# Hashed attention with spatial gating: the scores of two heads at once, each in 64 rows of the PE array, without copies of split q and k, and a part of the last batch's feed-forward sums moved ahead

## The chip, the cores and the metric

The kernel runs on one core of a Trainium2 chip. Its engines work side by side, each through its own instructions in order: TensorE (PE, with its weight loads shown apart as PEld), VectorE (DVE), ScalarE (ACT), GpSimd (POOL) and SyncE (SP), which here only issues DMAs. The time is device microseconds for one execution; lower is better. A profile is one execution taken apart.

## The reference, cut to what matters

```python
# attention: B=4, H=8, S=768, D=64
q_bucket, k_bucket = sign bits of q @ proj, k @ proj        # 6 bits each
mask = q_bucket[:, :, :, None] == k_bucket[:, :, None, :]
scores = where(mask, q @ k.T / 8, -1e9)
attn = softmax(scores)                                      # over the keys
x = (attn @ v) of all heads, side by side                   # B x 768 x 512
# feed-forward with spatial gating: d_ff = 1024
h = relu(x @ w_in);  u, v = halves of h
v_n = (v - mean(v)) / sqrt(var(v) + 1e-6)
v_s = w_spatial @ v_n + b_spatial                           # over the sequence
out = (u * v_s) @ w_out
```

## The kernel before, in words

Precision is kept by splitting: q, k, v, x and the weights each become a float16 high part and a float16 rest, and a product is made of three float16 products (high by high, high by rest, rest by high). The mask is part of the score product: the six hash bits of a query and a key and their complements are extra rows of the contraction, scaled so that a key of another bucket gets a score far below the others.

The work is counted in heads n = 0 to 31 (two heads are a pair p = n // 2, eight heads a batch) and in row tiles i = 0 to 5 of 128 rows. One head step g = 6n + i is one row tile of one head.

For each pair q and k are loaded (`load_qk`, L149), the hash bits are made by four matmuls in four column strips of the array (`hash_rows`, L168), and the split parts are written to `hl` (`split_qk`, L185), with the two heads of the pair in partitions 0 to 63 and 64 to 127. `build` (L193) then copies, by DMA, the parts of one head into a tile `ab` of its own, so that all 128 rows are used in a contraction: one matmul takes the rest of q over the high part of q, against the high part of k over the rest of k, and the other takes the high parts over the hash rows. The big copies (L199, L205, L211, L212) go to SP's queue, the small ones of the hash bits (L201) to SP's for the first batch and to ACT's queue later.

`scores` (L278) does a head step for queries in rows: four matmuls of 384 columns into a PSUM tile of two banks (L291, L292), the row minimum of the negated scores on DVE (L293), the exponential on ACT (L295), the split of the result into `pp` (L298 on ACT, L299 on DVE or POOL), and a DMA transpose to `pt` on SP's queue (L301). Heads 1 to 7 (`KEYS`, L451) instead have the keys in rows (`scores_k`, L256), which needs no transpose; for that the row maxima are found ahead of time (`row_max`, L235: two matmuls and a maximum on DVE) and put into the hash rows. The PSUM pool for both, `ps_sc` (L67), holds two tiles. `weighted` (L303) multiplies by v a few head steps later (`LAG` 5, `LAGK` 3), `normalize` (L318) ends a head, and `transpose_x` (L341) turns the pair's result into `xt`.

When a batch's eight heads are done, `mlp_units` (L350) puts 28 units in a queue: six for v, then for each half of the sequence four for u, four for the spatial product s and three for the output. Each unit is one PSUM tile of 12 or 18 matmuls. The main loop (L504 to L569) takes 28 units from the queue over 48 head steps of the next batch; after the last head step, the rest is emitted in a row (L572). The weights are converted bit by bit over the first 73 head steps (`W_PTS`, L456).

The order on each engine is set by the scheduler, from the priorities that `at(g, k)` (L485) gives to what is emitted.

Of the kernel before, what the change touches and what calls it, by code (L numbers as in the profile page):

```python
# [19 lines left out]
P = 128  # L20
# [16 lines left out]
def lsh_attention_spatial_gating(  # L37
# [22 lines left out]
    VYB = 2  # L60
# [21 lines left out]
    NAB = 4  # L82
    NR = D + 2 * NB
    ab = [const.tile([P, 4, S], F16, name=f"ab{i}") for i in range(NAB)]
    for i, t in enumerate(ab):
        eng = nc.vector if i % 2 else nc.gpsimd
        eng.memset(t[D:P, 2:4, :], 0.0)
        eng.memset(t[96:P, 2, :], HK)
# [76 lines left out]
    def has_keys(p):  # L165
        return 2 * p in KEYS or 2 * p + 1 in KEYS

    def has_queries(p):  # L168
        return not (2 * p in KEYS and 2 * p + 1 in KEYS)

    def hash_rows(p):
# [11 lines left out]
        st["sg", p] = s1  # L183

    def split_qk(p):  # L185
        qk = st["qk", p]
        hl = wk.tile([P, 4, S], F16, tag="hl", bufs=1, name=f"hl{p}")
# [4 lines left out]

    def build(n):  # L193
        p, e = divmod(n, 2)
        hl, sg, t = st["hl", p], st["sg", p], ab[n % NAB]
        r = slice(D * e, D * e + D)
        q_s, q_h = (BQ_S[n >= NH], BQ_H[n >= NH])
        if n < 1:
            nc.sync.dma_start(out=t[0:D, 2:4], in_=hl[r, 1:3])  # L199
        for j in range(4):  # L200
            q_s.dma_start(  # L201
                out=t[D:NR, 3 - j // 2, (j % 2) * HS:(j % 2 + 1) * HS],
                in_=sg[32 * j + 16 * e:32 * j + 16 * e + 2 * NB, :])
        if n < 1:
            q_h.dma_start(out=t[0:D, 0:2], in_=hl[r, 0:2])  # L205
        else:

            top = hl[r, 0:2]
            (ps, pn), (ss, sn), (es, en) = top.ap
            src = replace(top, ap=[(ps, pn), (ss, 2), (ss, 2), (es, en)])  # L210
            q_h.dma_start(out=t[0:D].rearrange("p (a b) s -> p a b s", b=2), in_=src)  # L211
        q_h.dma_start(out=t[D:P, 0:2], in_=hl[r, 2:4])  # L212
# [8 lines left out]
    def mean_v(p):  # L221
# [6 lines left out]
        nc.gpsimd.tensor_add(c, c, a[:, 4:6])  # L228
        mp = ps_m.tile([P, 512], F32, tag=MT, name=f"mp{p}")
# [5 lines left out]
    def row_max(n, i):  # L235
        t = ab[n % NAB]
        if i == 0:
            st["mx", n] = wk.tile([P, NT], F32, tag="mx", bufs=2, name=f"mx{n}")
        ps = ps_sc.tile([P, 2, 512], F32, tag="sc", name=f"mp{n}_{i}")[:, :, :HS]
        for c in range(2):  # L240
            nc.tensor.matmul(ps[:, c], lhsT=t[0:P - 1, 3, i * P:(i + 1) * P],
                             rhs=t[0:P - 1, 2, c * HS:(c + 1) * HS], start=True, stop=True)
        nc.vector.reduce_max(st["mx", n][:, i:i + 1], ps, axis=AX.XY)
        if i == NT - 1:
            nb = st["nb", n] = wk.tile([P, NT], F32, tag="nb", bufs=3, name=f"nb{n}")
# [8 lines left out]
            MQ.dma_start(out=t[P - 1:P, 3, :], in_=mt)  # L254

    def scores_k(n, i):  # L256
        t = ab[n % NAB]
        ps = ps_sc.tile([P, 2, 512], F32, tag="sc", name=f"sp{n}_{i}")[:, :, :HS]
        ks = slice(i * P, (i + 1) * P)
        for c in range(2):  # L260
            cs = slice(c * HS, (c + 1) * HS)
            nc.tensor.matmul(ps[:, c], lhsT=t[:, 1, ks], rhs=t[:, 0, cs], start=True, stop=False)  # L262
            nc.tensor.matmul(ps[:, c], lhsT=t[:, 2, ks], rhs=t[:, 3, cs], start=False, stop=True)  # L263
        ex = wk.tile([P, S], F32, tag="pt", bufs=PTB, name=f"ex{n}_{i}")
        st["ex", n, i] = nc.scalar.activation(ex.rearrange("p (c q) -> p c q", c=2), ps, AF.Exp, scale=ISQ).ins
        st["pt", n, i] = ex
# [11 lines left out]
    def scores(n, i):  # L278
        if n in KEYS:
            scores_k(n, i)  # L280
            return
        t = ab[n % NAB]
        if i == 0:
            st["nb", n] = wk.tile([P, NT], F32, tag="nb", bufs=3, name=f"nb{n}")
        nb = st["nb", n][:, i:i + 1]
        jk = wk.tile([P, 2, HS], BF16, tag="jk", name=f"jk{n}_{i}")
        qs = slice(i * P, (i + 1) * P)
        ps = ps_sc.tile([P, 2, 512], F32, tag="sc", name=f"sp{n}_{i}")[:, :, :HS]
        for c in range(2):
            cs = slice(c * HS, (c + 1) * HS)  # L290
            nc.tensor.matmul(ps[:, c], lhsT=t[:, 0, qs], rhs=t[:, 1, cs], start=True, stop=False)  # L291
            nc.tensor.matmul(ps[:, c], lhsT=t[0:P - 1, 3, qs], rhs=t[0:P - 1, 2, cs], start=False, stop=True)  # L292
        nc.vector.tensor_scalar(jk, ps, -ISQ, None, op0=ALU.mult, op1=ALU.min, accum_out=nb)  # L293
        ex = wk.tile([P, 2, HS], F32, tag="ex", bufs=EB, name=f"ex{n}_{i}")
        st["ex", n, i] = nc.scalar.activation(ex, ps, AF.Exp, bias=nb, scale=ISQ).ins  # L295
        at(NT * n + i + G_H, 50)
        pp = wk.tile([P, 2, 2, HS], F16, tag="pp", bufs=PB, name=f"pp{n}_{i}")
        nc.scalar.copy(pp[:, 0], ex)  # L298
# [4 lines left out]
    def weighted(n, i):  # L303
        if n in KEYS:
            weighted_k(n, i)
            return
# [307 lines left out]
```

## Time and profile before

| | us |
|---|---|
| median of 3 runs | 740.14 (740.12 to 741.45) |
| the profiled execution | 743.49 |
| its span, first to last instruction | 741.7 |
| PE, DVE, ACT, POOL busy in it | 631.5, 520.6, 434.8, 321.2 |

Busy time is the union of an engine's instructions. PE's matmuls overlap, and each is shown with its latency, so that a busy PE need not be at its peak. The granted clock is the share of TensorE's full clock that it was given. The chain of waits is followed back from the last instruction to what released it at each step. A line of a group reads: line, engine, operation, output<-input, shapes, count, then busy time in all, the mean in ns, and the idle time ahead of it with what ended that. DMAs in the chain are named by output<-input.

### The profile page before, as it was taken

To read this page: it belongs to the slowest core of one execution; us is meant where nothing else is said; L and a number is where in the kernel's file an instruction comes from. 1 tells how busy PE (TensorE), PEld (TensorE's weight loads), DVE (VectorE), ACT (ScalarE), POOL (GpSimd) and SP (SyncE) were. 2 spreads that over 40 slices of the span, in tenths; PEclk is the share of its full clock that TensorE was granted. 3 is DMA by queue.
4 is the path that set the end of the run, shared out by engine and by line. 5 is a ranking of instruction groups with operands and counts; after the bars stand their busy time and mean duration, and the time that the engine had idled before them with its cause. 6 is when DMAs were issued, how large, how long until landed. Compare 5 with 4: busy or idle time off the path is not lost.

```text
span 741.7 us, 14927 instructions
## 1 busy us (share of the span) xinstructions
PE 631.5 (85%) x5759; PEld 400.4 (54%) x5759; DVE 520.6 (70%) x945; ACT 434.8 (59%) x668; POOL 321.2 (43%) x324
## 2 busy tenths in 40 slices
PE   1569898998988776997898899889898998999997
PEld 0237686776445444554544555556455565654553
DVE  4677795536799999567689798678698987755200
ACT  1344574346788676655676577667677776743221
POOL 5122443123458675264314565156235571451503
PEclk9768797999999989898999999999999999999999
DMA  9565554324999989996999799999999999860011
GB/s 235 149 123 155 133 148 102 99 55 97 224 237 197 215 207 187 213 178 138 234 202 199 138 210 213 211 211 212 206 210 181 194 175 213 182 136 15 1 42 43
DMA packets 290011, 120.95 MB, mean 163 GB/s; under 512 B 270740, under 2 KB 273812, under 8 KB 289940
## 3 DMA queue, kind: packets, MB, share of 16 engines
q1 hardware_dynamic: 287636, 119.11, 76.4%
q10 hardware_dynamic: 2304, 0.89, 0.5%
q8 instruction: 45, 0.74, 0.4%
q14 instruction: 26, 0.21, 0.1%
HBM read 28.33 MB, written 6.29 MB: 47 GB/s over the span
## 4 chain that ended last, share of the span: by engine, by line
PE 43%; DMA 21%; DVE 13%; issue 8%; ACT 6%; POOL 6%; SPq 3%; ACTq 0%; DVEq 0%; POOLq 0%
DMA pt<-pp 14%; PE pv L275 6%; PE vps L361 6%; PE ops L432 5%; PE sps L417 5%; PE ups L402 5%; DMA ab<-hl 4%; PE sp L291 3%; DVE jk L293 3%; PE sp L292 3%; DVE pp L299 2%; PE sp L262 2%; PE pv L314 2%; ACT ex L295 2%; PE sp L263 2%
## 5 line engine op out<-in xcount | busy, mean ns | idle before, releaser
L295 ACT ACTIVATE ex<-sp,nb 128x768 f32<-128x768 f32 x150 | 134.1, 897 | 54.8 <-DVE jk L293 48.9
L299 DVE TENSOR_TENSOR pp<-ex,pp 128x768 f16<-128x768 f32 x116 | 126.2, 1089 | 47.6 <-ACT pp L298 46.5
L293 DVE TENSOR_SCALAR_CACHE_REDUCE jk<-sp 128x768 bf16<-128x768 f32 x150 | 142.4, 949 | 24.1 <-PE sp L292 22.2
L298 ACT CAST pp<-ex 128x768 f16<-128x768 f32 x150 | 124.3, 829 | 50.0 <-DMA pt<-pp 43.9
L314 PE MATMUL pv<-vp,pt 128*128 128x65 f16 x900 | 108.2, 198 | 40.5 <-DMA pt<-pp 40.2
L291 PE MATMUL sp<-ab 128*128 128x384 f16 x300 | 103.2, 344 | 31.6 <-ACT ex L295 19.3
L314 PEld LDWEIGHTS <-pt 128*128 128x128 f16 x900 | 86.7, 101 | 67.2 <-DMA pt<-pp 53.4
L299 POOL TENSOR_TENSOR pp<-ex,pp 128x768 f16<-128x768 f32 x34 | 58.1, 1708 | 131.1 <-ACT pp L298 124.6
L315 PE MATMUL pv<-vp,pt 128*128 128x64 f16 x900 | 108.0, 197 | 0.0
L316 PE MATMUL pv<-vp,pt 128*128 128x65 f16 x900 | 107.8, 198 | 0.0
L292 PE MATMUL sp<-ab 127*128 127x384 f16 x300 | 103.9, 346 | 0.0
L417 PE MATMUL sps<-ws,vn 128*128 128x384 f16 x576 | 100.9, 329 | 1.5 <-DVE sg L180 1.0
L315 PEld LDWEIGHTS <-pt 128*128 128x128 f16 x900 | 87.0, 100 | 11.3 <-issue 1.3
L316 PEld LDWEIGHTS <-pt 128*128 128x128 f16 x900 | 86.9, 100 | 3.1 <-issue 0.5
L417 PEld LDWEIGHTS <-vn 128*128 128x128 f16 x576 | 55.3, 99 | 37.8 <-issue 3.9
L432 PE MATMUL ops<-wo,g 128*128 128x512 f16 x288 | 70.9, 391 | 1.5 <-ACT o L436 0.9
L275 PEld LDWEIGHTS pv<-vf,ex 128*128 128x128 f32 x504 | 68.5, 208 | 4.1 <-issue 1.6
L402 PE MATMUL ups<-xt,wi 128*128 128x384 f16 x384 | 69.1, 333 | 1.3 <-ACT u L405 0.9
L361 PE MATMUL vps<-wi,xt 128*128 128x512 f16 x288 | 68.0, 383 | 1.4 <-DMA xt<-xs 1.3
L275 PE MATMUL pv<-vf,ex 128*128 128x65 f32 x504 | 67.0, 286 | 0.0
L333 POOL TENSOR_TENSOR x<-x,xf 128x384 f32<-128x384 f32 x32 | 35.5, 1110 | 64.1 <-DVE x L332 64.1
L422 POOL TENSOR_TENSOR sy<-sy,u 128x384 f32<-128x384 f32 x32 | 36.6, 1145 | 49.3 <-DVE sy L421 49.2
(87 smaller groups left out, 1010.7 us busy)
## 6 DMA issues: line engine op xcount, KB each, us to landing
qk<-kq SPq DMA_DIRECT2D x16, 768.0 KB
ab<-hl SPq DMA_DIRECT2D x31, 384.0 KB
ab<-hl SPq DMA_DIRECT2D x34, 192.0 KB
out<-o SPq DMA_DIRECT2D x24, 256.0 KB
v<-v SPq DMA_DIRECT2D x13, 384.0 KB
raw<-w_in SPq DMA_DIRECT2D x16, 256.0 KB
pt<-pp SPq DMA_TRANSPOSE x150
raw<-w_sp SPq DMA_DIRECT2D x12, 192.0 KB
```

The source lines that it names most:

```text
L275: nc.tensor.matmul(acc[:, qi, :], lhsT=ex[:, qi * P:(qi + 1) * P], rhs=vf[p % 2][:, 2 * i + e, :], start=(i == 0 and qi == 0), stop=(i == ...
L291: nc.tensor.matmul(ps[:, c], lhsT=t[:, 0, qs], rhs=t[:, 1, cs], start=True, stop=False)
L292: nc.tensor.matmul(ps[:, c], lhsT=t[0:P - 1, 3, qs], rhs=t[0:P - 1, 2, cs], start=False, stop=True)
L293: nc.vector.tensor_scalar(jk, ps, -ISQ, None, op0=ALU.mult, op1=ALU.min, accum_out=nb)
L295: st["ex", n, i] = nc.scalar.activation(ex, ps, AF.Exp, bias=nb, scale=ISQ).ins
L298: nc.scalar.copy(pp[:, 0], ex)
L299: (nc.gpsimd if i in (PL_POOL if n >= 2 * NH else PL_POOL1) else nc.vector).tensor_tensor(out=pp[:, 1], in0=ex, in1=pp[:, 0], op=ALU.subtract)
L314: nc.tensor.matmul(acc, lhsT=pt[:, c, :], rhs=vh, start=(i == 0 and c == 0), stop=False)
L315: nc.tensor.matmul(acc[:, 0:D], lhsT=pt[:, c, :], rhs=vl, start=False, stop=False)
L316: nc.tensor.matmul(acc, lhsT=pt[:, NT + c, :], rhs=vh, start=False, stop=(i == NT - 1 and c == NT - 1))
L361: nc.tensor.matmul(ps, lhsT=xt[c][:, gx, i * P:(i + 1) * P], rhs=wi[gw][:, c, F2:DF], start=(k == 0), stop=(k == 3 * NPAIR - 1))
L417: nc.tensor.matmul(ps[:, :HS], lhsT=vn[gv][:, c, d * P:(d + 1) * P], rhs=ws[gw][:, c, hs], start=(k == 0), stop=(k == 3 * NT - 1))
```

## The change

The unit of work becomes the pair: a pair step g = 6p + i is one row tile of both heads.

- `build` and the tiles `ab` go, with all copies of the split parts. A new function `sums` makes the scores straight from `hl`: four passes (rest by high, high by rest, high by high, hash) of 64 rows each, for the two heads in turn, the first head in partitions 0 to 63 and the second in 64 to 127, each into a PSUM tile of its own. `hl` gets three buffers. The hash rows lie in tiles `hk`, one for a pair with three in rotation, filled by eight small copies from `hash_rows`, on SP's queue (for pair 0 over the queues of SP, ACT and POOL).
- `scores`, `row_max`, `weighted` and `normalize` are called for both heads of a pair. `ps_sc` stays at two tiles; a pair step now takes both. The pairs with keys in rows are 1 to 3, so head 1 now has its queries in rows.
- The minimum's unused output is written into the exponential's tile. The normalised v is written in place.
- `partial_units`: once pair 14 is done, the sums of the last batch over its first three pairs are made for v (six units) and for the first half of u (four), of nine matmuls each, and copied to SBUF by ACT. The last batch's own units then need three matmuls for these, and DVE adds the copied part. In the last batch all of u comes before the first s, and its units take their PSUM tiles from `ps_m` and `ps_pv` in turn.
- Rates: 28 units over 24 pair steps as before, but 1.48 units per pair step in the last batch. The weights are converted by pair step 34. `LAG` is 3, `LAGK` 1, the row maxima lead by 8 pair steps; `pt` has 7 buffers for 5, `pp` and the exponentials 4 for 3.

The core of the diff:

```diff
-    NAB = 4
-    ab = [const.tile([P, 4, S], F16, name=f"ab{i}") for i in range(NAB)]
+    NHK = 3
+    hk = [const.tile([P, 2, S], F16, name=f"hk{i}") for i in range(NHK)]
...
     def hash_rows(p):
...
-        st["sg", p] = s1
+        for j in range(4):
+            for e in range(2):
+                HQS[(2 * j + e) % len(HQS) if p < 1 else 0].dma_start(
+                    out=hk[p % NHK][D * e:D * e + 2 * NB, 1 - j // 2, (j % 2) * HS:(j % 2 + 1) * HS],
+                    in_=s1[32 * j + 16 * e:32 * j + 16 * e + 2 * NB, :])
...
-    def build(n):
...
+    def sums(p, ps, rows, passes, queries):
+        for a, (x, y, last) in enumerate(passes):
+            for c in range(2):
+                cs = slice(c * HS, (c + 1) * HS)
+                for e in range(2):
+                    r = slice(D * e, D * e + D - (last and queries[e]))
+                    f = (lambda z: hk[p % NHK][r, z]) if last else (lambda z: st["hl", p][r, z])
+                    l, m = (x, y) if queries[e] else (y, x)
+                    nc.tensor.matmul(ps[e][:, c], lhsT=f(l)[:, rows], rhs=f(m)[:, cs],
+                                     start=(a == 0), stop=(a == len(passes) - 1))
+    ALL = ((0, 1, False), (2, 3, False), (2, 1, False), (1, 0, True))
...
+    def scores(p, i):
+        ps = [ps_sc.tile([P, 2, 512], F32, tag="sc", name=f"sp{p}_{i}_{e}")[:, :, :HS] for e in range(2)]
+        rows = slice(i * P, (i + 1) * P)
+        sums(p, ps, rows, ALL, (p not in KEYS,) * 2)
+        for e in range(2):
+            n = 2 * p + e
+            if p in KEYS:
+                ex = wk.tile([P, S], F32, tag="pt", bufs=PTB, name=f"ex{n}_{i}")
+                nc.scalar.activation(ex.rearrange("p (c q) -> p c q", c=2), ps[e], AF.Exp, scale=ISQ)
+                st["pt", n, i] = ex
+                continue
...
+            nc.vector.tensor_scalar(jk, ps[e], -ISQ, None, op0=ALU.mult, op1=ALU.min, accum_out=nb)
+            nc.scalar.activation(ex, ps[e], AF.Exp, bias=nb, scale=ISQ)
...
     def row_max(p, i):
+        ps = [ps_sc.tile([P, 2, 512], F32, tag="sc", name=f"mp{p}_{i}_{e}")[:, :, :HS] for e in range(2)]
+        sums(p, ps, slice(i * P, (i + 1) * P), ALL[2:], (True, True))
...
+    def partial_units():
+        p0 = NP - NPAIR
+        xt = [st["xt", p0 + r] for r in range(NPAIR - 1)]
+        vb = [wk.tile([P, 4, S], F16, tag="hl", bufs=3, name=f"vpart{j}") for j in range(2)]
+        ub = ld.tile([P, NF, HS], F32, tag="qk", bufs=QKB, name="upart")
...
+            for c in range(NPAIR - 1):
+                for t in THREE:
+                    nc.tensor.matmul(ps, lhsT=lhs(c, t), rhs=rhs(c, t), start=(k == 0), stop=(k == 3 * NPAIR - 4))
+                    k += 1
+            nc.scalar.copy(dst, ps)
...
         def v_unit(i):
-            ps = ps_m.tile([P, 512], F32, tag=MT, name=f"vps{b}_{i}")
+            ps = bank(f"vps{b}_{i}")
+            k0 = 3 * NPAIR - 3 if last else 0
...
+            if last:
+                nc.vector.tensor_tensor(out=v32[i], in0=ps, in1=st.pop(("vpart", i)), op=ALU.add)
+                ps = v32[i]
...
-                y = wk.tile([P, F2], F32, tag="vy", bufs=VYB, name=f"vy{b}_{i}")
+                y = v32[i]
...
-    KEYS = {1, 2, 3, 4, 5, 6, 7}
-    LAGK = 3
-    LEAD = 4
-    W_PTS = ((4, 0), (48, 16), (58, 22), (66, 29), (73, 37))
+    KEYS = {1, 2, 3}
+    LAGK = 1
+    LAG = 3
+    LEAD = 8
+    W_PTS = ((1, 0), (21, 16), (30, 28), (34, 37))
...
+            credit += 28.0 / STEPS if g < LASTB else LRATE
```

More of the change, by code (lines that the diff above doesn't have):

```diff
@@ L253, in row_max @@
             nc.vector.tensor_copy(mt, tp[0:NT, 0:P])
[L254 to L266, printed above, removed]
+            MQ.dma_start(out=hk[p % NHK][D * e + D - 1:D * e + D, 1, :], in_=mt)
     def weighted_k(n, i):
@@ L427, in o_unit @@
             h, j = divmod(i, NT // 2)
-            ps = ps_m.tile([P, 512], F32, tag=MT, name=f"ops{b}_{i}")
+            ps = bank(f"ops{b}_{i}")
             k = 0
```

280 lines of the change are left out of this document (136 added, 144 removed).

## The prediction

> **What bounds the kernel now.** I read the page's busy shares and its chain first, then busy time by stage, then the timeline of single steps.
>
> ```profile
> PE 631.5 (85%) x5759; PEld 400.4 (54%) x5759; DVE 520.6 (70%) x945; ACT 434.8 (59%) x668; POOL 321.2 (43%) x324
> ...
> PE 43%; DMA 21%; DVE 13%; issue 8%; ACT 6%; POOL 6%; SPq 3%; ACTq 0%; DVEq 0%; POOLq 0%
> DMA pt<-pp 14%; PE pv L275 6%; PE vps L361 6%; PE ops L432 5%; PE sps L417 5%; PE ups L402 5%; DMA ab<-hl 4%; PE sp L291 3%; DVE jk L293 3%; PE sp L292 3%; DVE pp L299 2%; PE sp L262 2%; PE pv L314 2%; ACT ex L295 2%; PE sp L263 2%
> ```
>
> No engine owns the chain: matmuls are two fifths of it, DMA one fifth, and of the DMA the transposes of the probabilities (pt) hold 14% of the span and the copies of split q and k (ab<-hl) 4%. To find the stages I took the first and last start of two kinds of instruction, then cut the span there.
>
> ```profile
> L262 PE MATMUL sp<-ab x84: 322/326/528, 51.4 to 170.7; 128*128 128x384 f16 x84
> ```
> ```profile
> L301 SPq DMA_TRANSPOSE pt<-pp x150: 1277/1605/3941, 28.7 to 655.7; - x150
> ```
> ```profile
> 21.00:51.00 30.00, 19.57 (x124) 10.29 (x121) 22.13 (x32) 11.85 (x15) 6.20 (x6) 0.66 0.58 140
> 51.00:171.00 120.00, 108.34 (x784) 86.55 (x784) 76.76 (x161) 60.98 (x107) 38.28 (x55) 0.89 0.45 114
> 171.00:656.00 485.00, 419.36 (x4347) 259.68 (x4346) 395.33 (x705) 335.66 (x500) 240.80 (x219) 0.95 0.98 196
> 656.00:742.00 86.00, 80.88 (x495) 43.34 (x492) 18.54 (x41) 22.26 (x44) 26.23 (x27) 0.99 0.13 40
> ```
>
> The columns are stretch, length, busy PE, PEld, DVE, ACT, POOL, granted clock, DMA share, GB/s. Head 0 takes 30 us; heads 1 to 7, which need no transposes, 120 us (42 steps, 2.86 us each); heads 8 to 31 take 485 us for 144 head steps, so 6.74 us per pair of heads and row tile, with the DMA share at 0.98; then a tail of 86 us in which DMA is idle and PE is dense. I call one pair of heads on one row tile a pair step. The 485 us are where the change matters most.
>
> **The middle stage, 72 pair steps.** First PE: what a matmul costs in a stream is the distance between starts, not its duration.
>
> ```profile
> 401.55 0.32 PE L291 MATMUL sp<-ab 128*128 128x384 f16 x1
> 401.55 0.10 PEld L292 LDWEIGHTS <-ab 127*128 127x128 f16 x1
> 401.71 0.33 PE L292 MATMUL sp<-ab 127*128 127x384 f16 x1
> ...
> 401.88 0.33 PE L291 MATMUL sp<-ab 128*128 128x384 f16 x1
> ```
> ```profile
> 404.67 0.19 PE L314 MATMUL pv<-vp,pt 128*128 128x65 f16 x1
> ...
> 404.70 0.19 PE L315 MATMUL pv<-vp,pt 128*128 128x64 f16 x1
> ```
>
> Score matmuls start 0.163 us apart, those of the weighted sum 0.03. Before, a pair step has 8 score matmuls over 128 rows: 1.30 us. After, it has 16 over 64 rows. If the two halves of the array run side by side they take 8 slots, 1.30 us again; if not, 2.6 us. No row of before has two row halves at work, but the hash has four column strips:
>
> ```profile
> 138.89 0.85 PE L175 MATMUL hp<-qk,hc 128*32 128x384 f32 x8
> 139.67 0.34 PE L262 MATMUL sp<-ab 128*128 128x384 f16 x1
> ```
>
> Eight records of 384 columns would take 8 x 0.163 = 1.30 us one behind the other even at the f16 rate; they took 0.78 until the next kind of matmul began, the change of array shape included. So strips do run together; the row nearest to the question says 1.30 us, and that is what I take.
>
> The weights are loaded twice as often. In the rows above, the load of L292 lies wholly within the matmul of L291 in the same rows, so I cost the loads at nothing; that cover ends only if a load must wait for its own half. The Trainium skill, "TensorE: Matmul & The Clock Gate", Part 3, says that a weight load overlaps matmuls in flight only where the row groups differ; the trace speaks against it here. By that rule each slot would be a tenth of a microsecond longer, the score work about 2.1 us, and my time below some 25 us later.
>
> PE per pair step is then 1.30 for scores, 36 x 0.03 = 1.1 for the weighted sums, 0.78/6 = 0.13 for the hash, and the feed-forward work. That is read from the tail, where it is alone:
>
> ```profile
> 666.62 15.54 PE vps L361 x72
> 682.16 7.80 PE ups L402 x48
> 689.96 11.70 PE sps L417 x72
> ```
>
> One batch has 15.5 (v) + 2 x 7.8 (u) + 2 x 11.7 (s) + 72 x 0.216 = 15.5 (out) = 70 us, over 24 pair steps 2.9. Sum 5.4 us, unchanged by the packing, against 6.74 used. DVE: 395.3/72 = 5.5 us; unchanged, since the minimum, subtraction and feed-forward passes stay.
>
> DMA is what loses work:
>
> ```profile
> ab<-hl SPq DMA_DIRECT2D x31, 384.0 KB
> ab<-hl SPq DMA_DIRECT2D x34, 192.0 KB
> ```
> ```profile
> L201 ACTq DMA_DIRECT2D ab<-sg x96: 726/736/2418, 147.5 to 609.5; - x96
> L201 SPq DMA_DIRECT2D ab<-sg x32: 713/722/1283, 12.7 to 113.0; - x32
> ```
> ```profile
> 477.50 9.48 DMA pt<-pp x2
> ```
>
> Each pair drops 2 x (384 + 192) KB = 1.18 MB, 0.197 MB per pair step, out of 196 GB/s x 6.74 us = 1.32 MB: 15%. At the present share the stage could run at 6.74 x 0.85 = 5.73 us. The last line is a transpose that took 9.5 us of the chain because two of these copies stood ahead of it in the same queue: that stall goes. What is late next is the feed-forward and score work on PE at 5.4 us.
>
> The eight hash copies of a pair move from ACT's queue to SP's: ACT's queue is freed of 8 x 0.736/6 = 1.0 us per pair step, SP gets 8 x 0.72/6 = 0.96 and loses four issues of the big copies. SP then has two transposes of 1.6 each, and some 0.5 of others: 4.7 us, below the rest. Behind a hash copy that waits for its bits stand that step's transposes; once in six steps, I cost it within the waits below.
>
> The change adds one dependence. The score pool has two tiles of PSUM; before, each head step took one, so one was filled while the other was read. Now a pair step takes both, and the matmuls alternate between them. The next scores wait for both exponentials.
>
> ```profile
> L295 ACT ACTIVATE ex<-sp,nb 128x768 f32<-128x768 f32 x150 | 134.1, 897 | 54.8 <-DVE jk L293 48.9 <-issue 3.2 <-DMA ab<-sg 0.7
> ...
> L293 DVE DVE_READ_ACCUMULATOR jk<-sp 128x1 f32 x150 | 12.2, 81 | 0.0
> ```
> ```profile
> L293 DVE TENSOR_SCALAR_CACHE_REDUCE jk<-sp 128x768 bf16<-128x768 f32 x150 | 142.4, 949 | 24.1 <-PE sp L292 22.2
> L299 DVE TENSOR_TENSOR pp<-ex,pp 128x768 f16<-128x768 f32 x116 | 126.2, 1089 | 47.6 <-ACT pp L298 46.5
> ```
>
> Matmuls 1.30, their end 0.2, two minima at 0.95 + 0.08 = 2.06, the second exponential 0.9, three hand-overs at 0.1: 4.75 us that can't overlap itself. Beside it PE has 4.1 us of other work, DVE 3.4; each is in order, so every hand-over can meet a pass of about 1 us (L299: 1.09) already started. Three such meetings at half a pass add 1.5: 6.25 us. The ends are 5.73 (DMA) and 6.74 (no gain) or above; I take 6.25, which is also their middle: 72 x 0.49 = 35 us less.
>
> **The first stage.** In steps without transposes the order is:
>
> ```profile
> 141.95 0.33 PE L262 MATMUL sp<-ab 128*128 128x384 f16 x1
> ...
> 142.60 1.45 PE L275 MATMUL pv<-vf,ex 128*128 128x65 f32 x12
> 142.86 0.81 ACT L265 ACTIVATE ex<-sp 128x768 f32<-128x768 f32 x1 [1.51 <-PE sp L263]
> ...
> 144.21 0.33 PE L262 MATMUL sp<-ab 128*128 128x384 f16 x1
> ```
> ```profile
> L243 DVE TENSOR_REDUCE mx<-mp 128x1 f32<-128x768 f32 x42 | 39.8, 952 | 23.3 <-PE mp L241 23.2
> ```
>
> The best head step is 2.26 us, all PE; the mean is 2.86, so a pair costs 5.7. After, scores (1.3 + 0.2 + 2 x 0.81 + 0.2 = 3.3) and row maxima (0.65 + 0.2 + 2 x 0.95 + 0.2 = 2.95) take turns on the same two tiles: 6.3, with 1.0 for meetings 7.3, in the ten steps that have both; 4.2 in the eight that have only scores (PE: 1.3 + 2 x 1.28). That is 107 us for three pairs against 18 x 5.7 = 103. Pair 0, now wholly with transposes, has 4.75 + 2.95 + 1.5 = 9.2 per step, 55 us; before, heads 0 and 1 took 30 + 6 x 2.86 = 47.
>
> ```profile
> 12.73 8.36 SPq L201 DMA_DIRECT2D ab<-sg  x8
> ```
> ```profile
> 21.09 0.50 PE L292 MATMUL sp<-ab 127*128 127x384 f16 x1
> ```
>
> The first scores waited until 21.1 for eight hash copies on one queue; on three queues, 4 us less. Stage: +4 +8 -4 = +8 us (estimate, from -5 to +25).
>
> **The tail.** Of the last batch, v needs 3 matmuls for 12 and the first half of u 3 for 12: 15.5 x 3/4 + 7.8 x 3/4 = 17.5 us of PE leave it. Moved forward they lie in the last three steps, where no other feed-forward unit is left (6.25 - 2.5 free in each), and under the last transposes; batch 2's units are hurried for this to 1.48 per step, PE 1.30 + 1.1 + 0.13 + 1.48 x 2.5 = 6.2 us, just below my 6.25. Without that cover the saving is lost.
>
> ```profile
> L390 POOL TENSOR_TENSOR vn<-vy,vn 128x512 f16<-128x512 f32 x24 | 30.9, 1300 | 40.7 <-ACT vn L389 40.7
> ...
> L369 DVE BATCH_NORM_STATS2 bs<-vr 128x6 f32<-128x512 f32 x24 | 16.5, 686 | 13.4 <-ACT vr L365 13.4
> ```
>
> Given back: the normalisation has only v 3.9 + u 2.0 + 7.8 = 13.7 us of PE to hide behind, while six units of an added sum (put at 0.6), statistics (0.69) and their aggregation (0.2), and then three last POOL passes (1.3), with v's four buffers held till then, reach about 16: 2.5 us. Normalising two heads at the very end instead of one: put at 2 (nought to 4). Net -13 us.
>
> **Sum.** The profiled execution took 743.49 us, its span 741.7, so 1.8 lies around it; it stands 3.35 over the median of 740.14. 743.5 - 35 + 8 - 13 = 703.5, against the median 700.
>
> **The rivals.** (1) PSUM takes over from DMA: the 4.75 us chain, with more than 2.05 us of waits per pair step, is above 6.8 and the sum turns positive. For it: DVE's other 3.4 us may all fall inside the chain; L293 and L295 already wait for each other (22.2 and 48.9 us). Against: priorities put scores first. At 7.1: +26, first stage +12, tail -13: 765. The Trainium skill, "TensorEngine Tiling (Array Packing)", Gotcha 1, warns that row tiles raise the PSUM pressure since each writes its own bank. Chance 0.15. (2) The halves do not run together: PE 6.7 per pair step, chain 6.05 and waits: 7.3, +40; first stage +50; tail -13: 817. Against it the hash rows. 0.05. (3) Full relief, waits under 1 us: 5.73, -73, first stage 0, tail -15: 652. PE at 5.4 and DVE at 5.5 leave little room for it. 0.1. The forecast has 0.7.
>
> **How the numbers follow.** The forecast's own spread is 0.4 us per pair step (29 us) and the first stage's ends; about 668 to 738, which leaves out (2), most of (1) and the far end of (3). Faster takes in (3) and the forecast less its upper edge: 0.78. Within 0.2%, 1.5 us, about what a measurement of this kernel can tell from no change, lie that edge and the near edge of (1): 0.04. Slower is the rest of (1) with (2): 0.18.
>
> **What would show it.** Right: score matmuls of the two halves starting within hundredths of a microsecond, 0.16 between couples; no ab<-hl issues; pair steps near 6.25 in the middle; v in the tail at about 4 us of PE; key steps slower than before wherever row maxima run. Wrong: couples 0.16 apart within; score matmuls waiting for ACT's exponentials for over 2 us per pair step; DMA share still 0.98 at the old pace.

## The result, and the profile after

The changed kernel took 894.99 us (median of 4 runs, 894.10 to 896.50) against 740.80 for the kernel before: the ratio is 1.2122, with a 95% interval from 1.2062 to 1.2183. The profiled execution took 894.64 us, its span 892.9. Against 741.7 before, that is 151 us more. (The kernel before has one run more here than in the table above, 743.72 us, so its median is another.) Some runs of the kernels tested below fell in a slower state of the chip, so their ratios leave those runs out and their medians don't.

The page of the changed kernel, busy shares and chain of waits:

```profile
PE 829.5 (93%) x6622; PEld 474.9 (53%) x6622; DVE 528.1 (59%) x963; ACT 445.9 (50%) x684; POOL 308.0 (34%) x328
...
PE 12%; DVE 1%; POOL 1%; DMA 0%; issue 0%; ACT 0%; ACTq 0%; POOLq 0%
```

PE is busy 198 us longer than before and now for 93% of the span; DVE and ACT hardly changed. The chain adds up to 14%: it reaches back to 759 us only and says nothing of what lies before. For those I cut the span again, at the first key exponential, the last one, and the last weighted sum. The rows of these tiles, then the stretches (same columns as in the prediction), of the changed kernel:

```profile
L277 ACT ACTIVATE ex<-sp x36: 790/810/811, 91.2 to 280.2; 128x768 f32<-128x768 f32 x36
```
```profile
L311 PE MATMUL pv<-vp,pt x936: 191/194/262, 27.1 to 822.7; 128*128 128x65 f16 x188
```
```profile
30.00:91.00 61.00, 57.15 (x333) 26.66 (x331) 40.45 (x71) 25.26 (x37) 13.53 (x17) 1.00 0.45 100
91.00:281.00 190.00, 186.07 (x808) 117.54 (x806) 59.56 (x114) 54.00 (x93) 30.66 (x45) 1.00 0.18 49
...
280.20:822.70 542.50, 508.50 (x5070) 292.86 (x5070) 390.43 (x707) 336.48 (x503) 226.17 (x219) 0.96 0.81 152
```

Cut at the same events, the kernel before has its last key exponential at 171.3 and its last weighted sum at 660.4. So the first stage, all that lies before the last key exponential, grew from 171 to 280 us (+109), the middle from 489.1 to 542.5 (+53: 7.53 us per pair step for 6.79), and what follows shrank from 81.3 to 70.2 (-11). DMA has let go, with a share of 0.81 for 0.97. In the first stage and in the middle it is PE that is full (186 of 190 us in the key steps, 508.5 of 542.5 in the middle).

What fills it in the middle is seen in the timeline of one pair step of the changed kernel:

```profile
498.94 1.13 PE L230 MATMUL sp<-hl 64*128 64x384 f16 x6 [0.96 <-ACT ex L286]
499.91 0.49 PE L230 MATMUL sp<-hk 63*128 63x384 f16 x2
...
500.98 1.14 PE L230 MATMUL sp<-hl 64*128 64x384 f16 x6
501.97 0.49 PE L230 MATMUL sp<-hk 63*128 63x384 f16 x2
```

The six matmuls of the first group use up 499.91 - 498.94 = 0.97 us, 0.16 each: they belong to one head, in one half of the array, one behind the other. Then come weighted sums, then the other head's eight. In the order of TensorE's instructions only 240 of the 840 possible couples stand side by side. Where a block of one half directly follows a block of the other, these overlap too (e3 below): in the trace 333 times two of the 1,680 score and row-maximum matmuls start within 0.08 us of each other. That makes 1,347 slots, 905 of them in the middle for its 1,152 matmuls, or 12.6 per pair step, 2.05 us at 0.163. The program writes the two heads in turn; the scheduler doesn't keep that, as I read it because the PSUM tile of the first head comes free about a microsecond ahead of the second's, so that the matmuls of the one are ready while those of the other still wait. The PSUM was not what they waited for in the main, as the group on the page shows (12.4 us in all):

```profile
L230 PE MATMUL sp<-hl 64*128 64x384 f16 x1152 | 222.4, 374 | 14.4 <-ACT ex L286 12.4
```

In the first stage something else is added:

```profile
239.68 2.12 PE L266 MATMUL pv<-vf,ex 128*128 128x65 f32 x9
241.74 2.10 PE L230 MATMUL sp<-hl 64*128 64x384 f16 x6
243.63 0.84 PE L230 MATMUL sp<-hk 64*128 64x384 f16 x2
```

Six matmuls now use 243.63 - 241.74 = 1.89 us, 0.315 each: TensorE runs at half its clock. The window's row shows a granted clock of 1.00 there, which can't be: this trace has no record of the clock before 265.6 us, and the column reads 1.00 where there is none. The other three runs of the kernel have a mean clock of 0.87, this one 0.973. In e11 below, the same kernel without the partial sums, the same stretch has the same count of matmuls and a clock of 0.50 (first row; second row, the changed kernel):

```profile
200.00:220.00 20.00, 20.00 (x81) 12.84 (x80) 3.05 (x4) 3.24 (x4) 0.47 (x2) 0.50 0.00 1
```
```profile
200.00:220.00 20.00, 20.00 (x81) 12.75 (x80) 3.05 (x4) 3.24 (x4) 0.47 (x2) 1.00 0.00 1
```

So the clock column has to be read beside the spacing of the matmuls, and the spacing decides. At half clock a key pair step is 16 x 0.315 + 24 x 0.229 (the nine f32 weighted sums above take 241.74 - 239.68 = 2.06 us) = 10.5 us of PE, row maxima and couples left aside; measured are 189/18 = 10.5.

### The profile page after: what moved, and what is told of

Its sections match the earlier page's. It is cut to its first block, busy times and chain, and to the rows that moved or that the text cites. A ratio compares the mean times of both kernels' runs of the same rounds, so it can differ in the third digit from the quotient of the medians.

```text
span 892.9 us, 16563 instructions
## 1 busy us (share of the span) xinstructions
PE 829.5 (93%) x6622; PEld 474.9 (53%) x6622; DVE 528.1 (59%) x963; ACT 445.9 (50%) x684; POOL 308.0 (34%) x328
## 5 line engine op out<-in xcount | busy, mean ns | idle before, releaser
L230 PE MATMUL sp<-hl 64*128 64x384 f16 x1152 | 222.4, 374 | 14.4 <-ACT ex L286 12.4
L285 DVE TENSOR_SCALAR_CACHE_REDUCE ex<-sp 128x768 bf16<-128x768 f32 x156 | 145.7, 951 | 47.9 <-PE sp L230 47.5
L230 PEld LDWEIGHTS <-hl 64*128 64x128 f16 x1224 | 93.3, 104 | 117.0 <-issue 75.3
L309 PE MATMUL pv<-vp,pt 128*128 128x65 f16 x936 | 110.7, 200 | 6.1 <-DMA pt<-pp 5.9
L309 PEld LDWEIGHTS <-pt 128*128 128x128 f16 x936 | 90.3, 102 | 37.1 <-issue 22.0
L311 PE MATMUL pv<-vp,pt 128*128 128x65 f16 x936 | 109.7, 201 | 0.0
L230 PE MATMUL sp<-hk 63*128 63x384 f16 (+1 forms) x384 | 99.4, 376 | 0.0
L311 PEld LDWEIGHTS <-pt 128*128 128x128 f16 x936 | 91.0, 101 | 12.6 <-issue 11.8
L310 PEld LDWEIGHTS <-pt 128*128 128x128 f16 x936 | 91.0, 101 | 9.7 <-issue 6.0
L266 PEld LDWEIGHTS pv<-vf,ex 128*128 128x128 f32 x432 | 82.7, 290 | 25.2 <-issue 24.0
L266 PE MATMUL pv<-vf,ex 128*128 128x65 f32 x432 | 89.6, 383 | 2.7 <-DVE x L327 2.7
L277 ACT ACTIVATE ex<-sp 128x768 f32<-128x768 f32 x36 | 28.3, 804 | 89.0 <-PE sp L230 89.0
L230 PEld LDWEIGHTS <-hk 63*128 63x128 f16 (+1 forms) x456 | 46.2, 114 | 44.8 <-issue 30.1
```

Source lines behind the costliest of these rows:

```text
L230: nc.tensor.matmul(ps[e][:, c], lhsT=f(l)[:, rows], rhs=f(m)[:, cs], start=(a == 0), stop=(a == len(passes) - 1))
L266: nc.tensor.matmul(acc[:, qi, :], lhsT=ex[:, qi * P:(qi + 1) * P], rhs=vf[p % 2][:, 2 * i + e, :], start=(i == 0 and qi == 0), stop=(i == ...
L285: nc.vector.tensor_scalar(jk, ps[e], -ISQ, None, op0=ALU.mult, op1=ALU.min, accum_out=nb)
L309: nc.tensor.matmul(acc, lhsT=pt[:, c, :], rhs=vh, start=(i == 0 and c == 0), stop=False)
L310: nc.tensor.matmul(acc[:, 0:D], lhsT=pt[:, c, :], rhs=vl, start=False, stop=False)
L311: nc.tensor.matmul(acc, lhsT=pt[:, NT + c, :], rhs=vh, start=False, stop=(i == NT - 1 and c == NT - 1))
```

## The experiments

My theory after the result had two causes: (1) the order separates the heads, so that the scores take far more than 8 slots; (2) half-row work leaves the clock low. The rivals were that the halves can't run together at all, that the PSUM of two score tiles is what holds the middle, and that DMA never bound it. Each row below is one profiled execution cut as above; "end" is from the last weighted sum to the end of the span; the median is of all timed runs, the ratio as said above.

| kernel | median us | ratio to before | first stage | middle | per pair step | end |
|---|---|---|---|---|---|---|
| before | 740.8 | 1 | 171 | 489 | 6.79 | 81 |
| changed | 895.0 | 1.212 | 280 | 542 | 7.53 | 70 |
| e1 one tile | 1004.5 | 1.356 | 254 | 683 | 9.48 | 68 |
| e4 one tile, no partial sums | 1019.4 | 1.377 | 260 | 673 | 9.35 | 81 |
| e5 turns | 881.4 | 1.200 | 240 | 566 | 7.86 | 70 |
| e6 turns, keys only | 874.1 | 1.190 | 240 | 564 | 7.83 | 69 |
| e7 turns, queries only | 940.8 | 1.281 | 301 | 566 | 7.86 | 71 |
| e8 before, with partial sums | 740.5 | 1.004 | 171 | 504 | 7.00 | 66 |
| e9 three passes | 861.8 | 1.169 | 274 | 520 | 7.22 | 71 |
| e10 idle matmuls | 871.9 | 1.184 | 263 | 538 | 7.47 | 71 |
| e11 no partial sums | 902.3 | 1.225 | 280 | 542 | 7.52 | 81 |
| e12 before, no copies | 717.7 | 0.975 | 159 | 476 | 6.61 | 82 |
| e13 before, one tile | 997.9 | 1.352 | 241 | 666 | 9.25 | 81 |
| e14 turns, three tiles | 885.7 | 1.196 | 222 | 544 | 7.55 | 121 |
| e15 its control | 943.9 | 1.271 | 269 | 579 | 8.05 | 96 |

**Do the halves run together, and at what clock? (e3)** A kernel of streams alone, 180 matmuls or more each, and of mixes:

```diff
+    def stream_one_half(t, b):
+        for i in range(200):
+            half(t, b, i, 0)
+    def stream_halves_in_turn(t, b):
+        for i in range(200):
+            half(t, b, i, 0)
+            half(t, b, i, 1)
+    def stream_halves_in_eights(t, b):
+        for i in range(200):
+            half(t, b, i, i // 8 % 2)
...
+    def mix_eights(t, b):
+        for n in range(10):
+            for e in range(2):
+                for i in range(8):
+                    half(t, b, i, e)
+                for i in range(6):
+                    wide(b, i)
```

> Streams of matmuls alone, each of some 40 us with an idle gap of 15 us ahead; the attention is left out and the output is a fill. In order: 200 on 128 rows; 200 on rows 0 to 63; 200 couples, halves in turn; 200 in eights, one half then the other; 180 float32 of 64 columns; then the mix of the key steps (8 score matmuls per head and 12 float32) with the halves in eights, in turn, and on 128 rows. C1: the full clock is reached on 128 rows and with the halves in turn (0.16 us a slot), and never with one half alone or in eights (0.32); among the mixes only the second and third reach it. C2: all streams without gaps reach 0.16 after some us. Rival B: halves in turn take 0.16 each, so 64 us instead of 32 for 200 couples.

Timeline of this kernel, one row for a stream; the last rows are the mix of the key steps (scores and f32 weighted sums), first in eights, then in turn:

```profile
57.86 64.18 PE L41 MATMUL b<-gate 64*128 64x384 f16 x200 [15.71 <-ACT gate L110]
137.75 34.80 PE L41 MATMUL b<-gate 64*128 64x384 f16 x400 [15.71 <-ACT gate L110]
188.27 19.92 PE L41 MATMUL b<-gate 64*128 64x384 f16 x200 [15.72 <-ACT gate L110]
224.76 77.06 PE L45 MATMUL b<-vt,qk 128*128 128x64 f32 x360 [16.57 <-ACT vt L97]
...
417.50 2.82 PE L45 MATMUL b<-vt,qk 128*128 128x64 f32 x12
420.25 2.74 PE L41 MATMUL b<-gate 64*128 64x384 f16 x8
...
467.76 1.47 PE L41 MATMUL b<-gate 64*128 64x384 f16 x16
469.16 2.89 PE L45 MATMUL b<-vt,qk 128*128 128x64 f32 x24
```
```profile
30.00:40.00 10.00, 10.00 (x63) 6.03 (x62) 0.00 (x0) 0.00 (x0) 1.00 0.00 0
80.00:90.00 10.00, 10.00 (x33) 4.63 (x32) 0.00 (x0) 0.00 (x0) 0.50 0.00 0
```

In turn, 400 take 34.8 us, which is 0.174 per couple including a cold start: the halves do run together. One half alone takes 0.32 per matmul and its clock stays at 0.50 through 64 us of work without a gap, where 128 rows are at 1.00 (the two windows). In blocks of eight without anything between, neighbouring blocks still overlap (0.10 each) and the clock rises too, where I had expected half the clock. The key mix in eights stays at half clock (eight in 2.74 us) through a hundred microseconds, and in turn it doesn't (sixteen in 1.47). The Trainium skill, "TensorE: Matmul & The Clock Gate", Part 1, says that about 3.4 us of sustained activity release the clock; here that holds for 128 rows in float16 and for both halves, and not for one half alone, nor for the float32 stream (360 records in 77.06 us, 0.214 each).

**Turns forced (e1, e4, e5, e6, e7).** e1 gives the two heads one PSUM tile of four banks, so that they become ready together; e4 is e1 without the partial sums; e5 chains the score and row-maximum matmuls of a pair in turns in the two tiles, e6 only for the key pairs (`p in KEYS` in place of `True`), e7 only for the others.

```diff
-    PSB = (2,2,2)
+    PSB = (1,2,2)
...
+        both = ps_sc.tile([P, 2, 2, 512], F32, tag="sc", name=f"sp{p}_{i}")
+        ps = [both[:, e, :, :HS] for e in range(2)]
```
```diff
-                for e in range(2):
+                for e in (1, 0):
...
+                        if before is not None and True:
+                            chain.enter_context(tc.issue_after(before))
+                        before = nc.tensor.matmul(ps[e][:, c], lhsT=f(l)[:, rows], rhs=f(m)[:, cs],
```

> Only change to the changed kernel: the two heads of a pair step share one PSUM tile of four banks instead of two tiles of two, so that neither head's matmuls can be ready before the other's. In the changed kernel only 240 of 840 couples of score matmuls stand half beside half in PE's order; here all 840 do. Theory A (the halves can run together, but the order of the program keeps them apart): score matmuls in couples 0.16 us apart, 8 slots of 1.3 us per pair step, middle stage near 6.3 us per pair step, total 700 to 760. With theory C1 (a matmul on half of the rows, alone, does not keep the clock up; two at once do) the first 280 us also shrink, to about 180. Rival B (halves do not run together in this kernel, whatever the order): no faster, 880 to 910, spacing 0.16 between the two of a couple. Rival C2 (the low clock of the first stage comes from PE waiting): the order helps but the first stage keeps half the clock, total about 800.

> The one-tile kernel without the early partial sums of the last batch (its units whole and in the old order, in the old PSUM pool). The prediction gave the partial sums 13 us (17.5 of PE moved, 4.5 given back): 13 us slower than the one-tile kernel. Rival: the moved work only delays the end of the attention, and the two are within 4 us.

> The changed kernel with its two PSUM tiles, but the score and row-maximum matmuls of a pair are queued one behind the other, second head first, half by half in turn; the first head's matmuls can then no longer start while the second head's tile is still read. 765 couples stand together in PE's order instead of 240. Theory A' (two separate losses: without turns no two halves at once and, in the first stage, half the clock; with turns no double buffering): first stage from 273 us down to about 200, middle stage 7.5 to 9 us per pair step because the chain matmuls, minima, exponentials can't overlap itself; total 880 to 980, between the changed kernel and the one-tile kernel, whose minimum of the second head also waited for the first head's exponential. Rival B' (the one-tile kernel was slow only for that extra wait): below 780.

> The same turns, but only for pairs 1 to 3 (their scores with keys in rows and their row maxima); the other pairs are left to the scheduler as in the changed kernel. C1: the first stage gets most of its clock back and ends about 60 to 90 us sooner; the middle is unchanged at 7.4 us per pair step; total 800 to 840. If the clock of that stage has another cause, its spacing stays at 0.32 and the total at 880 or more.

> The turns only for the pairs with queries in rows (pair 0 and 4 to 15). A': the first stage stays slow (half clock, 190 us for 18 pair steps); the middle costs 7.5 to 9 us per pair step, so the total is 900 to 1010. B': the middle falls to 6.3 us per pair step and the total to about 815.

Timeline of e1, the scores of one pair step:

```profile
600.23 1.15 PE L230 MATMUL sp<-hl 64*128 64x384 f16 x12
601.21 0.49 PE L230 MATMUL sp<-hk 63*128 63x384 f16 x4
```

Twelve use 0.98 us, 0.163 a couple, with both weight loads in it, and all 840 couples stand side by side. The prediction's 1.30 us per pair step is there, and yet e1 and e4 are the slowest of the five, far above the 700 to 760 us that I had expected of the couples. PE's busy time falls in e5 (718.9 for 829.5 us), and the first stage becomes 40 us shorter in e5 and e6, which both put turns into the key steps; for e6 I had expected 60 to 90. e7, without them, has it at 301. But the middle is 564 to 566 us in e5, e6 and e7 alike, 21 to 23 above the changed kernel. e6 has no turns in those steps, so the turns aren't what added it. What e5 to e7 share is the second head written first; I did not test that by itself. The couples gained nothing in the middle: e5 is no shorter there than e6, which starts far fewer couples together (514 and 295 in the traces). What rises with the turns is PE's wait for transposed probabilities, first in the middle of the changed kernel, then of e5:

```profile
PE pv L309 <- DMA pt<-pp: 4.6, 3, 2.9
```
```profile
PE pv L313 <- DMA pt<-pp: 60.3, 42, 4.7
```

The numbers are us in all, how often, and the longest.

**Is PE the bound of the middle? (e9)** One of the four score products of the queries is left out.

```diff
-        sums(p, ps, rows, ALL, (p not in KEYS,) * 2)
+        sums(p, ps, rows, ALL if p in KEYS else ALL[1:], (p not in KEYS,) * 2)
```

> The changed kernel, but the scores of the queries leave out one of their four products (the rest of q by the high half of k): 12 matmuls for 16 per pair step, one head behind the other as before, everything else unchanged. Theory A (the middle of the changed kernel is bound by TensorE, because its 16 score matmuls take 16 slots of 0.163 us): 72 pair steps x 4 x 0.163 = 47 us less, about 848 us, ratio to the kernel before about 1.15. Theory B (the middle is bound by the score pool's PSUM handing over, as when the halves take turns): no more than 10 us less, 885 or above.

The middle shrank by 23 us. The 312 matmuls left out broke up couples too: by the starts in the traces the slots fell by 180 (1,347 to 1,167), 175 of them in the middle (905 to 730), worth 175 x 0.163 = 29 us. So most of each slot saved comes back as time, as it would where PE is the bound; it is below the 47 expected, because fewer slots went. This run alone doesn't rule out the PSUM: each tile is also written for two matmuls less per step, 72 x 2 x 0.163 = 23 us. Against the PSUM stands that in the changed kernel those score matmuls waited for an exponential for 12.4 us in all.

**Is it the clock in the key steps? (e10)** Work over 128 rows is added, and its result not used.

```diff
+        idle = ps_m.tile([P, 512], F32, tag=MT, name=f"idle{n}_{i}")
+        for k in range(4):
+            nc.tensor.matmul(idle, lhsT=st["hl", p][:, 0, k * P:(k + 1) * P], rhs=st["hl", p][:, 1, 0:512], start=True, stop=True)
```

> The changed kernel with four idle matmuls of 128 rows by 512 columns added in each of the 36 key head steps, ahead of the weighted sum; their result is not used. Theory A (the key steps are slow because work that uses half of the rows does not raise TensorE's clock): the idle matmuls add 4 x 0.216 = 0.87 us per head step, but raise the clock; the key stage of 190 us falls to 125 to 155, the whole to 835 to 865 us. Theory B (the key steps are slow because of waits between the engines, the clock is no cause): the stage grows by 36 x 0.87 = 31 us or more (63 at half clock), the whole to 925 to 960 us.

Stretches of e10:

```profile
140.00:160.00 20.00, 20.00 (x69) 11.11 (x69) 3.17 (x7) 1.62 (x2) 0.71 (x3) 0.50 0.00 0
...
220.00:240.00 20.00, 20.00 (x145) 13.70 (x144) 5.15 (x11) 6.64 (x10) 4.81 (x5) 1.00 0.00 1
```

The key stage fell from 189 to 171 us (91.9 to 263.4) although 31 us of work at full clock was added. Up to about 175 us the clock stayed at 0.50 all the same; from there to the end of the stage it was 1.00, and PE did 145 matmuls in the time of 69. The direction is that of the clock theory, the size is short of the 125 to 155 that I expected, because four idle matmuls weren't enough in the first half of the stage; why not there is not shown.

**What does the PSUM cost? (e13, e14, e15)** e13 takes the second score tile from the kernel before, with no half-row work in it. e14 gives the turns of e5 a third score tile, for which the other two pools have one bank each; e15 has these single banks with two score tiles.

```diff
-    PSB = (2,2,2)
+    PSB = (1,2,2)
```
```diff
-    PSB = (2,2,2)
+    PSB = (3, 1, 1)
```
```diff
-    PSB = (2,2,2)
+    PSB = (2, 1, 1)
```

> The kernel before with one PSUM tile for scores instead of two, so that no head step's scores can be written while the step before is read; nothing else is changed, and no half of the array is used alone. It prices what a pair that takes both tiles loses. Theory A (the hand-over of PSUM is the reason why forced turns bring the middle to 7.75 us per pair step and one four-bank tile to 9.4): one head step can't be shorter than its matmuls 0.65, 0.2, minimum 1.03, exponential 0.9 and three hand-overs of 0.1, so 3.1 us, with meetings 3.6 to 4.5; the middle goes from 6.74 to 7.2 to 9 us per pair step, the whole to 775 to 900 us. Theory B (the turns cost time for another reason, PSUM has room): at most 10 us, 750 or less.

> The changed kernel with its score matmuls in turns of the two heads, and a third PSUM tile for scores, for which the pools of weighted sums and of all other matmuls have one bank each instead of two. To be read against the control with two score tiles and one bank each. Theory A (in turns, two score tiles leave no tile to fill while the pair is read): with a third the first head's scores of the next step can be begun; middle at least 0.4 us per pair step below the control's. Theory B (the room is not what limits the turns): no difference over 0.15 us per pair step.

> The control: the changed kernel with its score matmuls in turns and two PSUM tiles for scores as before, but one bank each for the pools of weighted sums and of all other matmuls. Both theories: slower than turns with two banks each (881 us), by an amount that is not known; 890 to 980 us. Only the difference to the kernel with three score tiles counts.

Groups of e13, its query exponentials and score matmuls:

```profile
L295 ACT ACTIVATE ex<-sp,nb 128x768 f32<-128x768 f32 x150 | 135.0, 900 | 204.4 <-DVE jk L293 199.2 <-DVE mv L370 3.4 <-DMA ab<-sg 1.5
...
L291 PE MATMUL sp<-ab 128*128 128x384 f16 x300 | 118.7, 396 | 84.3 <-ACT ex L295 68.9 <-DMA ab<-hl 10.1 <-DVE mx L243 5.2
```

Without the double buffer the kernel before loses 9.25 - 6.79 = 2.46 us per pair step, nearly as much as e1 (2.69 against before); at 998 us it came out above the 900 that I had put at most. ACT waits 199 us for the minimum where it waited 49, and PE 69 us for ACT where it waited 19. The idle PE also gets less clock (0.80 in this stage for 0.95). With a third tile the middle is 8.05 - 7.55 = 0.49 us per pair step shorter than in the control, but part of that is work put off. The spatial products behind the last weighted sum, of e14 and of e15:

```profile
L466 PE MATMUL sps<-ws,vn x216: 322/326/527, 765.5 to 873.8; 128*128 128x384 f16 x108
```
```profile
L466 PE MATMUL sps<-ws,vn x144: 326/326/326, 899.6 to 931.3; 128*128 128x384 f16 x144
```

e14 has 72 more of them there, and 24 more of the output's matmuls (108 for 84): 72 x 0.163 + 24 x 0.216 = 17 us of PE that the control did in the middle. The end is 25 us longer, and middle and end together are shorter by 579.3 + 95.7 - 543.6 - 121.1 = 10 us only, 0.14 per pair step. The first stage is 47 us shorter, at a granted clock of 0.80 for 0.68 in its key steps. So a third tile helps the turns in the key steps; that the room in PSUM is what limits them in the middle isn't shown. All eight banks are in use, so a third tile without single banks elsewhere is not to be had here. The Trainium skill, "TensorEngine Tiling (Array Packing)", Performance Considerations, says that tiling speeds up TensorE but not the emptying of PSUM; e1 agrees: its scores take 1.30 us per pair step, but a minimum 954 ns and an exponential 898, for 951 and 897 in the changed kernel.

**Was DMA the bound before? (e12)** The kernel before, with the copies of split q and k issued for the first four heads only.

```diff
+            if n < NAB:
                 q_h.dma_start(out=t[0:D].rearrange("p (a b) s -> p a b s", b=2), in_=src)
...
+        if n < NAB:
             q_h.dma_start(out=t[D:P, 0:2], in_=hl[r, 2:4])
```

> The kernel before, in which heads 4 to 31 issue no copies of split q and k into the operand tiles (768 KB and 384 KB per pair; their scores are taken of what the tiles hold from the first heads). Theory A (the middle of the kernel before is bound by DMA at a share of 0.98, so 15% less traffic gives 5.73 to 6.25 us per pair step): 72 x 0.49 to 72 x 1.0 less, 668 to 705 us. Theory B (the DMA share was high because the queues had waiting work, the pace is set by TensorE and VectorE): at most 10 us less, 730 to 740.

Stretches: the middle of the kernel before, then that of e12:

```profile
171.30:660.40 489.10, 423.32 (x4425) 262.49 (x4425) 396.36 (x706) 336.69 (x502) 243.96 (x222) 0.95 0.97 196
```
```profile
159.80:635.20 475.40, 422.66 (x4415) 261.86 (x4415) 395.82 (x705) 334.57 (x502) 253.70 (x221) 0.95 0.85 174
```

The DMA share fell from 0.97 to 0.85, and the middle by 13 us: 0.18 us per pair step, where I had counted 0.49 to 1.0. The first stage fell by 12. The ratio is 0.9753 (0.9696 to 0.9811), so the time lies between what the two theories gave.

**What are the early partial sums worth? (e8, e11)** e8 adds them alone to the kernel before, in free operand tiles and at the rate 0.74 per head step; e11 takes them out of the changed kernel.

```diff
+                    elif m == N - 3:
+                        queue += partial_units()
...
+            credit += 28.0 / DEN if g < LASTB else LRATE
```
```diff
-        last = b == B - 1
+        last = False
...
-                elif m == NP - 2:
-                    queue += partial_units()
```

> The kernel before with only the last part of the change: the last batch's sums over its first three pairs early, kept in two of the tiles ab that are free by then, its units in the new order and over two PSUM pools, and batch 2's units at 0.74 per head step. The prediction's tail alone: 13 us faster than before, about 725. Rival: in the last batch PE has less room than I took (6.7 us per pair of steps of which 6.2 are then used), the moved 17.5 us push the attention's end back, and the kernel is within 4 us of before.

> The changed kernel without the early partial sums of the last batch: its feed-forward work is all done behind the attention, as in the kernel before. Theory A (what moved forward lies beside a TensorE that is full already, so it is only moved): within 5 us of the changed kernel's 895. Theory B (the prediction's step: 17.5 us hidden, 4.5 given back): about 13 us slower, 908.

In the kernel before they gain nothing (ratio 1.0043, 0.9997 to 1.0089): the end shrinks by 15 us, and the middle grows by 15. In the changed kernel they do gain: without them the end is 80.7 for 70.2 us, the middle the same, the ratio 1.2254 for 1.2122, about 10 us, though the intervals just overlap (1.2179 to 1.2329, 1.2062 to 1.2183); in e4 against e1 15 us by the medians, with intervals that nearly touch. Rows of the changed kernel:

```profile
L358 PE MATMUL vpp<-wi,xt x54: 377/379/380, 807.9 to 826.4; 128*128 128x512 f16 x54
```

They run from 807.9 to 826.4, around the last weighted sum (822.7), as the prediction had it.

**No answer (e2).** Score and row-maximum matmuls over all 128 rows of `hl`, so that their output sums two heads.

```diff
-                    r = slice(D * e, D * e + D - (last and queries[e]))
+                    r = slice(0, P)
```

> The order of the changed kernel is kept, but every score and row-maximum matmul contracts all 128 rows, of both heads (scores are then sums over two heads, so the output is another one). Nothing can run side by side now. C1 (the clock follows how many rows are at work): the first stage gets the full clock back, spacing 0.16 instead of 0.32 us, and falls from 280 to about 190 us; the middle stays at 7.4 us per pair step; total about 810. C2 (the clock follows waits or the f32 matmuls): the first stage keeps 0.32 us and the total stays at 880 to 900.

One run took 4,228 us, with every kind of matmul slower: scores took 1,365 ns each, the output product of the feed-forward, which the edit doesn't touch, 1,700 for 384. It tells nothing of the halves, and what slowed all of TensorE there stays open.

## Why the prediction was wrong

The forecast of 700 us and its range to 738 were missed, and so were the rivals' 765 and 817. Of the 191 us between the sum of 703.5 and the profiled 894.6, 101 lie in the first stage, 88 in the middle and 2 in the tail.

**The step that failed** is the one that sets the score work: "16 over 64 rows ... they take 8 slots, 1.30 us again", with its premise, "the matmuls alternate between them". Its hardware half is right: e1 and e3 show couples at 0.163 to 0.174 us, weight loads included. (The Trainium skill's rule on weight loads, "TensorE: Matmul & The Clock Gate", Part 3, which the prediction weighed, isn't borne out here either: six matmuls of one half, each with its own load, start 0.16 us apart at 498.94.) Its software half is wrong: alternation in the program text is not alternation on the engine. In the middle the 16 matmuls take 12.6 slots, 2.05 us, so that PE needs 6.2 us per pair step with the prediction's other terms, for its 5.4: halfway to the 6.7 of rival (2), and for another reason than rival (2) gave. The pair step grew by about as much, from 6.79 to 7.53 us, and e9 shows that most of a slot saved comes back. What fills the rest, from 6.2 to 7.53, isn't split up; PE is idle for 0.47 of it (542.5 - 508.5 us in 72 steps). Nor would the right order alone have brought the forecast, as e5 shows.

**The first stage** was put at +8 us, at worst +25, and +50 in rival (2); it came to +109. The prices there, 1.3 us for the scores of a pair and 2 x 1.28 for its weighted sums, are those of the full clock, and the part nobody had in the sum is the clock: half-row scores with f32 weighted sums leave TensorE at half speed, 16 x 0.315 = 5.0 and 24 x 0.229 = 5.5, so 10.5 us per key pair step, 189 us for the 107 forecast. What lies ahead of the key steps took 91 us for 72 (17 to the first hash scores and 55 for pair 0). e3 shows it alone, e10 and e6 in the kernel. (The 4.2 for steps without row maxima also stands beside a sum that gives 3.9, worth under 3 us.) How the 109 us divide between slots and clock isn't separated exactly: turns in the key steps take back 40, idle matmuls 17 net.

**The PSUM chain** of 4.75 us with 1.5 us of waits was probably too short as well: with the order put right, in e5, the pair step is 7.86 us and not 6.25. Rival (1) had 7.1. A double buffer is worth 2.46 us per pair step in the kernel before (e13), where the prediction gave its loss three meetings at half a pass. That this is what makes e5 slow isn't shown, since e6, whose middle has no turns, takes 7.83.

**DMA.** "At the present share the stage could run at 5.73 us" failed too: the 15% less traffic is worth 0.18 us per pair step. A queue that is busy 98% of the time was taken for the bound. As I read it, its share was high because work was there to be moved, and PE and DVE set nearly the same pace. The 9.5 us that were quoted were also misread: the row holds two transposes, one issued at 477.50 and one from 481.45 on, and the two copies between them took 1.65 and 0.59 us to issue, so the copies were no more than a part of it.

**The tail** was right in mechanism, and its size close: -11 against -13. It depends on cover, as the prediction said: in the kernel before there is none (e8). Moving the hash copies to SP's queue cost little: PE waits 2.3 us for them in all. The start came sooner, as forecast: the first hash scores are at 15.6 us for 21.1.

## What to carry over

Work packed into parts of the array can gain only where the parts meet in the engine's own instruction order; look at that order, since a scheduler that goes by ready buffers can separate them when their buffers come free at different times. Look at the clock beside it, because work in one part alone may not raise it. Before a step is widened to two tiles, count the buffers: if it takes all of them, the overlap they gave is lost, and that can cost more than the packing saves. A high share of busy time on a queue is no bound until a run with less traffic is faster.

## What the runs showed of the hardware

- One half of the rows alone kept the granted clock at 0.50 for 64 us of dense work (0.32 us per matmul), and so did 128-row f32 matmuls of 64 columns (360 in 77.06 us, 0.214 each); both halves in turn, and 128-row f16, reached 1.00.
- Neighbouring blocks of eight of the two halves overlap too, if nothing stands between them: 200 matmuls in 19.92 us, 0.10 us each with the cold start.
- The clock column of a profile can be wrong for 200 us at a time: in the changed kernel it reads 1.00 where the spacing is 0.315 us, as long as the trace has no record of the clock (up to 265.6 us). The spacing of known matmuls tells.
